# Attention into two expert layers on one core: three token blocks beside each other while the dense weights are converted, instead of two

## The chip, the core and the metric

The program runs on one core of a Trainium2 chip. The core has five engines that run their own instruction lists in order and wait for each other by semaphores: TensorE (PE, matrix products into PSUM), VectorE (DVE), ScalarE (ACT), GpSimd (POOL) and SyncE (SP), which here only issues transfers. PSUM has eight banks of 128 x 512 fp32 values. The metric is the device time of one execution in microseconds, as the median of several runs.

## The reference

What is computed, cut to its core (sizes put in):

```python
# q, k, v: (8, 8, 576, 64) fp32
k_p, v_p = mean of 8 neighbouring rows of k and v          # 72 keys per head
attn = softmax(q @ k_p.T / 8);  a = attn @ v_p             # (8, 8, 576, 64)
x = a.transpose(0, 2, 1, 3).reshape(4608, 512)
h = x @ moe_w_in                                           # 512 -> 2048
x = maximum(0.01 * h, h) @ moe_w_out                       # 2048 -> 512
logits = x @ moe2_w_gate                                   # 8 experts
e = argmax(logits);  p = softmax(logits)[e]                # one expert a token
out[token] = p * (relu(x @ moe2_w1[e]) @ moe2_w2[e])
```

The dense weights `moe_w_in` and `moe_w_out` arrive as 64-bit floating point, everything else as fp32.

## The kernel before

The 4608 tokens are 18 **blocks** of 256 (`NB`, two tiles `t` of 128 each). For a block the dense layer has 16 **steps** `f` (`NF`): `g1(b, f)` makes 128 columns of h with 12 products of 256 columns (L426) into one of the PSUM banks called h, ScalarE writes 0.01 h to an SBUF tile `g` (L123), VectorE takes the maximum (the relu, L433) and writes it back over h in PSUM; `g_hi` (ScalarE) and `g_lo` (VectorE, L126) split it into a high and a low fp32r part in `ghl`; `g2(b, f)` multiplies these by 128 rows of the second weight with six products of 512 columns (L453) into the block's two accumulator banks called y. All products are done as three of such parts, for accuracy.

One entry (b, f) of the list `seq` is a **slot**; there are 288. In every slot the order on each engine is: `g1` of this slot, `g_lo` of the slot before (in the first part of the program), the slot's hooks (`run_slot`), `g2` of the slot two back, the weight conversion (`conv`), `g_hi`. Nothing reorders this: the order is written by hand (`manual_schedule`), and hooks are put into slots by `at(slot, function, ...)` and `plan()`.

**Weight conversion.** There are 32 pieces of raw weight of 512 KB, two kinds times 16 steps. `w_load64` fetches a piece into one of seven buffers `r64` on SP's queue. `w_conv1` takes two ScalarE steps (L391, L392) and four VectorE steps (L393, L396, L399, L402) to turn 64-bit words into fp32 words; `w_conv2` splits them with a ScalarE copy (L123) and a VectorE subtraction (L126) into the resident weight tiles w. Step f of a block needs pieces 2f and 2f+1, so the first blocks can go no faster than the pieces come. For this reason `seq` runs blocks 0 and 1 beside each other, block 1 four steps behind (`LAG`): slots 0 to 31 are these two, and block 2 starts at slot 32. Two pieces are converted per step of block 0, up to slot 25.

**Attention.** The tiles t = 0 to 35 go through `att_a` (transposes), `att_b` (scores and maximum), `att_e` (exp), `att_n` (normalise), `att_c` (transpose, split), and `att_av(b)` makes a block's x from two tiles. `kv_load`, `kv_pool` and `kv_use` prepare keys and values of a batch. Before the first slot tiles 0, 1 and batch 0 are done; tiles 2 and 3 stand in slots 0 to 3, batch 1 in slots 4 to 16, tiles 4 and 5 in slots 16 to 29, and `att_av(2)` in slot 31.

**PSUM.** Banks a0, a1 serve attention, the gate and all transposes (`pt("att")`); h0, h1 serve h; y0, y1 are the accumulators of block 0 and later of every block from 2 on; y2, y3 are those of block 1 and join the h banks in slot 38, step 6 of block 2.

**After a block.** `y_evac` copies the accumulators to the one tile `y4` and stores them; gate logits of block 0 come from TensorE (`y_tr` with eight transposes, `y_logit`), those of all others from VectorE (`logit`, 16 instructions L473 a block, on a table `wg` that is loaded when the start-up pool is closed at the end of block 1). `route_a`, `route_b`, `route_c` write the token lists. From slot 34 on, 128 chunks of the expert weights are split (`ps_load`, `ps_split`, `ps_store`), one every 1.8 slots. The expert layer follows the last slot.

Of the kernel before, what the change touches and what calls it, by code (L numbers as in the profile page):

```python
# [21 lines left out]
def kernel(  # L22
# [12 lines left out]
    nc = tc.nc  # L35
# [4 lines left out]
    LAG = 4  # L40
# [309 lines left out]
    def att_av(b):  # L350
        for g in range(2):
# [64 lines left out]
    w_raw, w_mid, w_cnt = {}, {}, [0]  # L416
# [395 lines left out]
    for i in range(NF + LAG):  # L812
        if i < NF:
            seq.append((0, i))
        if i >= LAG:
            seq.append((1, i - LAG))
    seq += [(b, f) for b in range(2, NB) for f in range(NF)]
# [6 lines left out]
    def plan():  # L824
        for t in range(4, NT // P):
# [34 lines left out]
        for b in range(NB - 1):  # L860
            s = (b + 1) * NF + 1
            lg_at = []
            if b == 0:
                at(30, y_evac, 0)
                at(31, y_tr, 0, 0)
                at(32, y_tr, 0, 1)
                at(33, y_logit, 0)
                r = (34, 36)
            elif b == 1:
                ev, r = 37, (46, 48)  # L870
                lg_at = [38 + j // 2 for j in range(16)]
# [31 lines left out]
    def y_tr(b, i):  # L903
# [3 lines left out]
        tg = (("qT", 1), ("q", 1))[i] if b == NB - 1 else ("kv", 2)  # L907
        yT[i] = sb([P, KD, P], F32, *tg)
# [11 lines left out]
    with tc.manual_schedule():  # L920
        stack = ExitStack()
        start = stack.enter_context(tc.tile_pool(name="start", bufs=1))
        x1 = start.tile([P, KD * 2 * BLK], F32R, name="x1")
        ebias = sb([P, 1], F32, "ebias")
        nc.vector.memset(ebias, -114688.0 * 65536.0)
        e_t = [start.tile([P, 512], U32, name=f"e{i}") for i in range(2)]
# [7 lines left out]
        x_of = {1: x1.rearrange("p (k h n) -> p k h n", k=KD, h=2)}  # L934
        w_todo = [(j, f) for f in range(NF) for j in range(2)]

        def xs(b):
            return x_of.get(b, x_v)

        def load2():  # L940
            for _ in range(2):
                if w_todo:
                    w_load64()
# [27 lines left out]
        w_conv1(0, 0)  # L971
# [179 lines left out]
```

## Time and profile before

| | us |
|---|---|
| median of 3 runs | 1569.42 (1568.0 to 1576.46) |
| the profiled execution, its own time | 1575.01 |
| its span, first to last instruction | 1573.2 |
| busy: PE, DVE, ACT, POOL in the span | 1478.4, 929.4, 643.2, 329.6 |
| granted TensorE clock, mean | 0.977 of full speed |

The page of the profile also cuts the span into 40 slices of 39.3 us. PE's busy tenths rise from 4 in the first slice to 9 in the eighth and stay there to the last but one; DVE's are 9, 8, 9 in the second to fourth slice, fall to 7, and are 8 up to the middle of the span. A matmul's busy time includes its way through the array, so the weight loads (PEld), which have no such overlap, are the better measure of how densely PE is fed. The expert layer takes the last third of the span with PE alone near its limit.

### The profile page before, as it was taken

To read this page: it belongs to the slowest core of one execution; us is meant where nothing else is said; L and a number is where in the kernel's file an instruction comes from. 1 tells how busy PE (TensorE), PEld (TensorE's weight loads), DVE (VectorE), ACT (ScalarE), POOL (GpSimd) and SP (SyncE) were. 2 spreads that over 40 slices of the span, in tenths; PEclk is the share of its full clock that TensorE was granted. 3 is DMA by queue.
4 is the path that set the end of the run, shared out by engine and by line. 5 is a ranking of instruction groups with operands and counts; after the bars stand their busy time and mean duration, and the time that the engine had idled before them with its cause. 6 is when DMAs were issued, how large, how long until landed. Compare 5 with 4: busy or idle time off the path is not lost. (4 is left out here: it accounts for less than half of the span.)

```text
span 1573.2 us, 25017 instructions
## 1 busy us (share of the span) xinstructions
PE 1478.4 (94%) x8778; PEld 1292.1 (82%) x8778; DVE 929.4 (59%) x2393; ACT 643.2 (41%) x1444; POOL 329.6 (21%) x290
## 2 busy tenths in 40 slices
PE   4567899999999999999999999999999999999998
PEld 3456689999898888899889899987888888888886
DVE  6989748978788879877878878653111111111111
ACT  4655544445444454544445444322222222222222
POOL 3000002232332233222222333021111111121111
PEclk8787999999999999999999999999999999999999
DMA  8533035656555555545636554054721331661160
GB/s 208 159 108 102 28 127 174 183 166 196 152 178 170 180 160 184 179 157 166 198 135 198 165 162 160 28 212 160 292 111 48 147 145 41 228 278 46 61 235 22
DMA packets 113280, 238.01 MB, mean 151 GB/s; under 512 B 47589, under 2 KB 55785, under 8 KB 109440
## 3 DMA queue, kind: packets, MB, share of 16 engines
q1 hardware_dynamic: 82208, 139.81, 28.5%
q10 hardware_dynamic: 23328, 76.56, 13.1%
q0 software_dynamic: 7616, 20.01, 3.9%
q8 instruction: 71, 1.16, 0.4%
q14 instruction: 57, 0.47, 0.2%
HBM read 418.44 MB, written 87.38 MB: 322 GB/s over the span
## 5 line engine op out<-in xcount | busy, mean ns | idle before, releaser
L453 PE MATMUL y<-w,ghl 128*128 128x512 f32 x1728 | 464.3, 406 | 0.4 <-DVE ghl L126 0.2
L453 PEld LDWEIGHTS y<-w,ghl 128*128 128x128 f32 x1728 | 311.0, 192 | 56.5 <-DVE ghl L126 1.7
L426 PEld LDWEIGHTS h<-x_t,w 128*128 128x128 f32 x1776 | 237.5, 196 | 58.9 <-issue 21.7
L426 PE MATMUL h<-x_t,w 128*128 128x256 f32 x1776 | 245.6, 289 | 40.8 <-ACT ghl L123 21.4
L126 POOL TENSOR_TENSOR ps<-ps 128x512 f32<-128x512 f32 x128 | 182.7, 1427 | 479.8 <-ACT ps L123 356.5
L473 DVE CUSTOM_DVE_ANT_0 junk<-y,wg 128x512 bf16<-128x512 f32 x256 | 197.9, 773 | 1.9
L426 PEld LDWEIGHTS y<-x_t,w 128*128 128x128 f32 x1488 | 189.6, 188 | 9.4
L426 PE MATMUL y<-x_t,w 128*128 128x256 f32 x1488 | 192.1, 280 | 0.0
L126 DVE TENSOR_TENSOR at_t<-a,at_t 128x512 fp32r<-128x512 f32 x76 | 52.4, 689 | 203.8 <-ACT at_t L123 203.6
L126 DVE TENSOR_TENSOR vm<-a,vm 128x512 fp32r<-128x512 f32 x40 | 27.7, 692 | 199.7 <-ACT vm L123 199.7
L123 ACT ACTIVATE g<-h 128x256 f32<-128x256 f32 x164 | 62.9, 383 | 173.0 <-PE h L426 162.4
L433 DVE TENSOR_TENSOR h<-g,h 128x256 f32<-128x256 f32 x164 | 69.5, 424 | 91.6 <-ACT g L123 91.0
L797 PE MATMUL y<-w,at_t 128*128 128x512 f32 x480 | 120.8, 400 | 1.4 <-ACT at_t L123 0.9
L805 POOL DMA_INDIRECT out_dram<-kv,sidx x40 | 40.3, 1008 | 382.7 <-ACT vm L123 192.3
L797 PE MATMUL y<-w,vm 128*128 128x512 f32 x480 | 120.3, 400 | 0.0
L771 PE MATMUL h<-w,x_t 128*128 128x512 f32 x480 | 118.5, 396 | 0.0
L771 PE MATMUL y<-w,x_t 128*128 128x512 f32 x480 | 118.4, 395 | 0.0
L123 ACT ACTIVATE ghl<-h 128x256 fp32r<-128x256 f32 x164 | 62.7, 382 | 111.3 <-PE y L453 46.7
L797 PEld LDWEIGHTS y<-w,at_t 128*128 128x128 f32 x480 | 88.6, 188 | 22.0 <-ACT at_t L123 1.2
L797 PEld LDWEIGHTS y<-w,vm 128*128 128x128 f32 x480 | 88.7, 188 | 20.1
L771 PEld LDWEIGHTS h<-w,x_t 128*128 128x128 f32 x480 | 88.7, 188 | 18.8 <-DVE x_t L126 0.4
L771 PEld LDWEIGHTS y<-w,x_t 128*128 128x128 f32 x480 | 88.6, 188 | 18.4
(238 smaller groups left out, 1906.4 us busy)
## 6 DMA issues: line engine op xcount, KB each, us to landing
w<-wsp SPq DMA_DIRECT2D x156, 2048.0 KB
wsp<-ps ACTq DMA_DIRECT2D x128, 512.0 KB
ps<-in_moe_w_dram SPq DMA_DIRECT2D x128, 256.0 KB
y_d<-y ACTq DMA_DIRECT2D x18, 512.0 KB
q<-in_q_dram SPq DMA_DIRECT2D x28, 256.0 KB
kv<-in_k_dram SPq DMA_DIRECT2D x24, 288.0 KB
kv<-in_v_dram SPq DMA_DIRECT2D x24, 256.0 KB
ps<-in_moe_w_in_dram SPq DMA_DIRECT2D x8, 512.0 KB
```

What stands on the lines that cost most here:

```text
L123: nc.scalar.activation(o, i, AF.Copy, scale=scale)
L126: eng.tensor_tensor(out=o, in0=a, in1=b, op=ALU.subtract)
L426: nc.tensor.matmul(p[:, 0:BLK], win(f)[:, kk, l], xv[:, kk, r], start=(n == 0), stop=(n == 3 * KD - 1))
L433: nc.vector.tensor_tensor(out=g, in0=t, in1=g, op=ALU.max)
L453: nc.tensor.matmul(y_ps[b, i], hl[:, l, i * P:i * P + P], wout(f)[:, r], start=(f == 0 and l + r == 0), stop=(last and l == 1),)
L473: nc.vector.tensor_tensor_reduce(out=jk, in0=y_sb[b][:, i], in1=wg_t[0][:, e], scale=1.0, scalar=0.0, op0=ALU.mult, op1=ALU.add, accum_out ...
L771: nc.tensor.matmul(p, xT2[:, t % 2, kk, l], wlane(lane(t), fh * KD + kk)[:, r], start=(n == 0), stop=(n == 3 * KD - 1))
L797: nc.tensor.matmul(p, d[:, kk, l], wlane(lane(t), 2 * KD + 4 * j + kk)[:, r], start=(j == 0 and n == 0), stop=(j == 1 and n == 11),)
L805: nc.gpsimd.indirect_dma_start(out=out, out_offset=bass.IndirectOffsetOnAxis(ap=sidx[:, t:t + 1], axis=0), in_=o, in_offset=None, bounds_c ...
```

## The change

- `seq` holds three blocks beside each other (`NQ = 3`), each three steps behind the other (`LAG = 3`): slot 9 + 3(i - 6) begins step i from 6 to 15, with (0, i), (1, i - 3), (2, i - 6). The 48 slots of three blocks are slots 0 to 47. Pieces are converted two per step of block 0, now up to slot 34, and the second of a pair goes one slot later than the first.
- Block 2 has its own x tile (`x2`), and its accumulators are a0, a1. So from slot 11 to 39 there is no bank for attention: tiles 4 and 5, all of batch 1 and `att_av(2)` are moved up to slots 1 to 10. After block 0 is evacuated (slot 39) `pt("att")` uses y0, y1. Blocks from 3 on accumulate in y2, y3, and a0, a1 join the h banks at slot 50.
- In blocks 0 to 2 the relu is written to the SBUF tile `g` instead of back to PSUM, and `g_hi`, `g_lo` read it there.
- The raw weights have five buffers instead of seven. The conversion's `e` tiles move into `y4`.
- Blocks 0, 1 and 2 are evacuated in slots 39, 46 and 48, and all three get their logits from TensorE (tile `yT` in `x1`'s place). The start-up pool is closed at slot 54, the table `wg` loaded then. Expert chunks start at slot 38 instead of 34.

```diff
-    LAG = 4
+    LAG = 3
+    NQ = 3
...
         t = sb([P, BLK], F32, "g", 2)
-        g = p[:, 0:BLK]
-        act_copy(t, g, 0.01)
-        nc.vector.tensor_tensor(out=g, in0=t, in1=g, op=ALU.max)
+        h = p[:, 0:BLK]
+        g = t if b < NQ else h
+        act_copy(t, h, 0.01)
+        nc.vector.tensor_tensor(out=g, in0=t, in1=h, op=ALU.max)
...
-                y_ps[b, i] = bank(f"y{2 * (b == 1) + i}")
+                y_ps[b, i] = bank(("y0", "y1", "y2", "y3", "a0", "a1")[2 * min(b, 2) + i] if b < NQ else f"y{2 + i}")
...
+    for i in range(NF + (NQ - 1) * LAG):
+        seq += [(b, i - b * LAG) for b in range(NQ) if 0 <= i - b * LAG < NF]
+    seq += [(b, f) for b in range(NQ, NB) for f in range(NF)]
...
+        for t, ss in ((4, (5, 6, 6, 7, 8)), (5, (7, 8, 8, 9, 10)), (6, (40, 41, 42, 42, 44)), (7, (42, 43, 44, 45, 46))):
+            for fn, c in zip((att_a, att_b, att_e, att_n, att_c), ss):
+                at(c, fn, t)
+            at(ss[0], q_load, t + 1)
+        at(10, att_av, 2)
+        at(47, att_av, 3)
...
+            if b < NQ:
+                e = (44, 47, 50)[b]
+                if b < NQ - 1:
+                    at((39, 46)[b], y_evac, b)
+                at(e, y_tr, b, 0)
+                at(e + 1, y_tr, b, 1)
+                at(e + 2, y_logit, b)
+                r = (e + 3, e + 5)
...
-        r64.append(sb([P, 1024], I32, "y4"))
-        r64.append(start.tile([P, 1024], I32, name="r64"))
         r64 += [sb([P, 1024], I32, "kv", 2) for i in range(2)]
...
+        def conv2(n):
+            w_conv2(n % 2, n // 2)
+            if n + 5 < 2 * NF:
+                w_load64(n + 5)
...
-        for i, c in enumerate((6, 8, 10, 12, 14, 15, 16)):
-            at(c - 2, kv_pool, 1, i)
+        for i, c in enumerate((2, 3, 4, 5, 6, 7, 8)):
+            at(c - 1, kv_pool, 1, i)
             at(c, kv_use, 1, i)
...
+        for n in range(2, 2 * NF):
+            c = slot[0, n // 2 - 1] + (n % 2 if n >= 2 * LAG + 2 else 0)
+            cv_at.setdefault(c, []).append(n)
...
-            if (b, f) == (2, 6):
-                banks["h"] += ["y2", "y3"]
+            if (b, f) == (NQ, 2):
+                banks["h"] += ["a0", "a1"]
...
+            if s == slot[0, NF - 1] + 3:
+                banks["att"] = ["y0", "y1"]
+            if (b, f) == (NQ, 6):
                 stack.close()
```

TensorE in the middle of the conversion. Before, slots of block 0 (x_t, accumulators y0 and y1) and block 1 (x1, y2 and y3) take turns:

```order
L426 MATMUL h1_997<-x_t_67,w02_872 128x256 x12
L453 MATMUL y0_508<-w12_907,ghl_958 128x512 x2
L453 MATMUL y1_509<-w12_907,ghl_958 128x512 x2
L453 MATMUL y0_508<-w12_907,ghl_958 128x512
L453 MATMUL y1_509<-w12_907,ghl_958 128x512
L426 MATMUL h0_1039<-x1_102,w01_572 128x256 x12
L453 MATMUL y2_748<-w11_576,ghl_995 128x512 x2
L453 MATMUL y3_749<-w11_576,ghl_995 128x512 x2
L453 MATMUL y2_748<-w11_576,ghl_995 128x512
L453 MATMUL y3_749<-w11_576,ghl_995 128x512
```

After, at the same place (the six products have the line number 454 there):

```order
L426 MATMUL h1_1048<-x_t_67,w01_611 128x256 x12
L454 MATMUL y2_756<-w10_324,ghl_1021 128x512 x2
L454 MATMUL y3_757<-w10_324,ghl_1021 128x512 x2
L454 MATMUL y2_756<-w10_324,ghl_1021 128x512
L454 MATMUL y3_757<-w10_324,ghl_1021 128x512
L426 MATMUL h0_1083<-x1_102,w01_611 128x256 x12
L454 MATMUL a0_1100<-w10_324,ghl_1046 128x512 x2
L454 MATMUL a1_1101<-w10_324,ghl_1046 128x512 x2
L454 MATMUL a0_1100<-w10_324,ghl_1046 128x512
L454 MATMUL a1_1101<-w10_324,ghl_1046 128x512
L426 MATMUL h1_1120<-x2_103,w00_292 128x256 x12
```

A third block (x2, accumulators a0 and a1) has come between the two, with 18 more products per step.

VectorE at the same places. Before, every slot of this part holds a relu, a lo subtraction and one conversion (and pooling of batch 1 in some):

```order
L433 TENSOR_TENSOR h_884<-g,h_884 128x256
L126 TENSOR_TENSOR ghl<-h_842,ghl 128x256
L126 TENSOR_TENSOR w_907<-y_111,w_907 128x512
L393 SCALAR_TENSOR_TENSOR e_106<-kv,e_106 128x512
L396 TENSOR_SCALAR kv<-kv 128x512
L399 SCALAR_TENSOR_TENSOR kv<-kv 128x512
L402 TENSOR_TENSOR kv<-kv,e_106 128x512
L433 TENSOR_TENSOR h_919<-g,h_919 128x256
L126 TENSOR_TENSOR ghl<-h_884,ghl 128x256
```

After (relu L434, subtractions L127):

```order
L434 TENSOR_TENSOR g<-g,h_1083 128x256
L127 TENSOR_TENSOR ghl<-g,ghl 128x256
L127 TENSOR_TENSOR w_1108<-ps,w_1108 128x512
L393 SCALAR_TENSOR_TENSOR y_106<-kv,y_106 128x512
L396 TENSOR_SCALAR kv<-kv 128x512
L399 SCALAR_TENSOR_TENSOR kv<-kv 128x512
L402 TENSOR_TENSOR kv<-kv,y_106 128x512
L434 TENSOR_TENSOR g<-g,h_1120 128x256
L127 TENSOR_TENSOR ghl<-g,ghl 128x256
L434 TENSOR_TENSOR g<-g,h_1145 128x256
L127 TENSOR_TENSOR ghl<-g,ghl 128x256
```

Two slots of three hold a conversion, the third holds a relu and a lo subtraction only; the relu writes g, and the pooling has gone from here.

SP's queue at the start, raw weight pieces (L379, L381) among the loads of batch 1. Before:

```order
L379 DMA r_112<-in_moe_w_in_dram 128x4x256
L198 DMA w_328<-in_k_dram 72x4x512 x2
L381 DMA kv<-in_moe_w_out_dram 128x1024
L205 DMA w_332<-in_v_dram 64x4x512 x2
L210 DMA w_332<-in_v_dram 8x512 x8
L379 DMA kv<-in_moe_w_in_dram 128x4x256
```

After:

```order
L379 DMA kv<-in_moe_w_in_dram 128x4x256
L381 DMA ps<-in_moe_w_out_dram 128x1024
L379 DMA ps<-in_moe_w_in_dram 128x4x256
L199 DMA w_328<-in_k_dram 72x4x512 x2
L206 DMA w_331<-in_v_dram 64x4x512 x2
L211 DMA w_331<-in_v_dram 8x512 x8
```

Two pieces that reuse a buffer (ps) now stand ahead of the keys and values of batch 1; each of the two waits for the conversion that empties its buffer.

## Rows read from the trace of the kernel before

**Rows 1.** Four stretches: each engine's busy time (instructions), granted clock, DMA share, GB/s.

```profile
43.13:102.81 59.68, 35.87 (x174) 30.77 (x175) 54.33 (x106) 34.18 (x66) 0.00 (x0) 0.79 0.43 134
102.81:181.60 78.79, 59.60 (x326) 49.99 (x324) 73.14 (x146) 48.87 (x100) 2.56 (x4) 0.88 0.27 84
181.60:269.10 87.50, 84.06 (x569) 75.58 (x569) 56.41 (x168) 35.50 (x85) 12.41 (x9) 1.00 0.38 123
269.10:323.01 53.91, 53.10 (x362) 48.70 (x362) 44.78 (x115) 27.72 (x70) 15.56 (x12) 1.00 0.58 170
```

**Rows 2.** Timeline of DVE (start, duration, instruction, idle before): relus of slots 0, 48.

```profile
43.13 0.42 DVE L433 TENSOR_TENSOR h<-g,h 128x256 f32<-128x256 f32 x1
...
269.10 0.43 DVE L433 TENSOR_TENSOR h<-g,h 128x256 f32<-128x256 f32 x1 [1.27 <-ACT g L123]
```

**Rows 3.** Waits of DVE, 43 to 182 us: total, times, longest.

```profile
DVE h L433 <- ACT g L123: 4.3, 3, 3.5
```

**Rows 4.** Waits of PE, 43 to 182 us.

```profile
PE h L426 <- ACT ghl L123: 21.4, 9, 3.3
```

**Rows 5.** Waits of PE's weight loads, 182 to 270 us.

```profile
PEld h L426 <- DVE ghl L126: 5.4, 6, 2.0
```

**Rows 6.** Timeline of DVE, slot 7 before: relu, lo, conversion, next relu.

```profile
99.03 0.42 DVE L433 TENSOR_TENSOR h<-g,h 128x256 f32<-128x256 f32 x1
...
99.69 0.68 DVE L126 TENSOR_TENSOR w<-kv,w 128x512 fp32r<-128x512 f32 x1
100.30 0.68 DVE L393 SCALAR_TENSOR_TENSOR e<-ps,e 128x512 uint32<-128x512 uint32 x1
...
102.81 0.42 DVE L433 TENSOR_TENSOR h<-g,h 128x256 f32<-128x256 f32 x1
```

**Rows 7.** Timeline of DVE: attention's steps n and b, then c, of two tiles.

```profile
52.09 0.74 DVE L322 TENSOR_REDUCE st<-pr 128x8 f32<-128x576 f32 x1
...
54.06 0.45 DVE L312 TENSOR_REDUCE w<-a 128x4 f32<-128x288 f32 x1
...
55.77 0.68 DVE L126 TENSOR_TENSOR w<-r,w 128x512 fp32r<-128x512 f32 x1
...
62.67 0.68 DVE L126 TENSOR_TENSOR at_t<-a,at_t 128x512 fp32r<-128x512 f32 x1
...
63.83 0.75 DVE L322 TENSOR_REDUCE w<-w 128x8 f32<-128x576 f32 x1
```

**Rows 8.** All pooling (L225) in the conversion stretch: busy time of DVE, POOL, clock, DMA.

```profile
43.13:181.60 138.47, 9.26 (x21) 0.00 (x0) 0.84 0.34 105
```

**Rows 9.** Groups of DVE instructions, 40 to 185 us: values' low parts.

```profile
L253 DVE SCALAR_TENSOR_TENSOR vm<-w,vm 64x128 fp32r<-64x128 f32 x4 | 1.1, 282 | 0.0
```

**Rows 10.** Timeline of DVE: first subtraction of att_av(2) in slot 31.

```profile
206.23 0.69 DVE L126 TENSOR_TENSOR x_t<-a,x_t 128x512 fp32r<-128x512 f32 x1 [1.22 <-ACT x_t L123]
```

**Rows 11.** Timeline of PE's weight loads: one slot with nothing else, 186.08 to 189.21.

```profile
186.08 1.59 PEld L426 LDWEIGHTS h<-x_t,w 128*128 128x128 f32 x12
187.61 1.23 PEld L453 LDWEIGHTS y<-w,ghl 128*128 128x128 f32 x6
189.21 0.89 PEld L426 LDWEIGHTS h<-x,w 128*128 128x128 f32 x7 [0.37 <-DVE ghl L126]
```

**Rows 12.** Timeline of PE's weight loads: transposes, logits of block 0, scores of a tile.

```profile
212.18 0.47 PEld L906 LDWEIGHTS a<-ident,y 128*128 128x128 f32 x4
...
215.40 1.87 PEld L915 LDWEIGHTS a<-wgk,kv 128*128 128x128 f32 x16
...
218.56 1.04 PEld L306 LDWEIGHTS a<-kT,qT 128*128 128x128 f32 x8
```

**Rows 13.** Timeline of ACT and DVE: a conversion's ScalarE steps, then DVE's first step.

```profile
36.08 0.66 ACT L123 ACTIVATE w<-ps 128x512 fp32r<-128x512 f32 x1
...
37.33 0.72 ACT L392 ACTIVATE e<-junk,ebias 128x512 uint32<-128x512 uint16 x1
...
38.09 0.69 DVE L393 SCALAR_TENSOR_TENSOR e<-ps,e 128x512 uint32<-128x512 uint32 x1 [0.31 <-ACT e L392]
```

**Rows 14.** DMA in 105.56 to 109.0 us: one raw piece, issued at 105.56.

```profile
DMA packets 144, 0.52 MB, mean 152 GB/s; under 512 B 16, under 2 KB 16, under 8 KB 144
```

More of the change, by code (lines that the diff above doesn't have):

```diff
@@ L453, in g2 @@
             nc.tensor.matmul(
-                y_ps[b, i], hl[:, l, i * P:i * P + P], wout(f)[:, r], start=(f == 0 and l + r == 0),
+                y_ps[b, i], hl[:, l, i * P:i * P + P], wout(f)[:, r], start=(first and l + r == 0),
                 stop=(last and l == 1),
@@ L790, in m_g2 @@
         if j == 0:
-            o_ps[t] = bank(f"y{t % 2}")
+            o_ps[t] = bank(f"y{2 + t % 2}")
         p = o_ps[t]
@@ L811 @@
     seq = []
[L812 to L817, printed above, removed]
+    for i in range(NF + (NQ - 1) * LAG):
+        seq += [(b, i - b * LAG) for b in range(NQ) if 0 <= i - b * LAG < NF]
+    seq += [(b, f) for b in range(NQ, NB) for f in range(NF)]
+    slot = {x: s for s, x in enumerate(seq)}
     NSLOT = len(seq)
@@ L824, in plan @@
     def plan():
-        for t in range(4, NT // P):
+        for t, ss in ((4, (5, 6, 6, 7, 8)), (5, (7, 8, 8, 9, 10)), (6, (40, 41, 42, 42, 44)), (7, (42, 43, 44, 45, 46))):
[4 more added lines that the diff above has]
+        at(47, att_av, 3)
+        for t in range(8, NT // P):
             b, i = divmod(t, TPB)
@@ L834, in plan @@
             at(s + 5, att_c, t)
-        for b in range(2, NB):
+        for b in range(4, NB):
             at((b - 1) * NF + NF - 1, att_av, b)
@@ L862, in plan @@
             lg_at = []
[L863 to L871, printed above, removed]
+            if b < NQ:
[6 more added lines that the diff above has]
+                r = (e + 3, e + 5)
             elif b == NB - 2:
-                ev, r = None, (s + 9, s + 11)
+                r = (s + 9, s + 11)
                 lg_at = [s + j // 2 for j in range(16)]
             else:
-                ev, r = None, (s + 15, s + 19)
+                r = (s + 15, s + 19)
                 lg_at = [s + max(j - 1, 0) for j in range(16)]
-            if b == 1:
-                at(ev, y_evac, b)
             for j, x in enumerate(lg_at):
@@ L906, in y_tr @@
             nc.tensor.transpose(p[:, kk * P:kk * P + P], y_sb[b][:, i, kk * P:kk * P + P], ident)
-        tg = (("qT", 1), ("q", 1))[i] if b == NB - 1 else ("kv", 2)
-        yT[i] = sb([P, KD, P], F32, *tg)
+        if b == NB - 1:
+            yT[i] = sb([P, KD, P], F32, ("qT", "q")[i])
+        else:
+            if i == 0:
+                yT["both"] = start.tile([P, TPB, KD, P], F32, name="yT", tag="x1")
+            yT[i] = yT["both"][:, i]
         act_copy(yT[i], p.rearrange("p (k n) -> p k n", k=KD))
@@ L933, with conv1 @@
         alt = sb([P, 4096], F32, "w02")
[L934 to L943, printed above, removed]
+        for b, x in ((1, x1), (2, x2)):
+            x_of[b] = x.rearrange("p (k h n) -> p k h n", k=KD, h=2)
+        def conv1(n):
+            w_conv1(n % 2, n // 2)
+        def conv2(n):
+            w_conv2(n % 2, n // 2)
+            if n + 5 < 2 * NF:
+                w_load64(n + 5)
         kv_load0_k(0)
@@ L948 @@
         kv_load0_v(0)
-        load2()
-        load2()
+        for n in range(4):
+            w_load64(n)
         q_load(2)
         q_load(3)
-        w_load64()
+        w_load64(4)
         consts()
```

83 lines of the change are left out of this document (38 added, 45 removed).

## The prediction

> **What bounds the kernel now.** I read the program by stretches, cut where VectorE starts a slot's relu [rows 1, 2]. In the first two (slots 0 to 7 and 8 to 23) DVE is busy 54.3 of 59.7 us and 73.1 of 78.8 us, PE's weight loads only 30.8 and 50.0. Whether DVE is the bound, the waits say: from 43 to 182 us it waits 4.3 us in all for a relu's input [rows 3], while PE waits 21.4 us for h banks that ScalarE still reads [rows 4]. So 24 slots take 138.5 us, the pace of the conversion on DVE. From 181.6 us on it is PE: weight loads 75.6 of 87.5 us, clock 1.00, and the waits left are 5.4 us, for an h bank that VectorE's lo subtraction still reads [rows 5]. The conversion stretch is where PE has room; the total of products in the program hardly changes, so what the change can win is PE's idle time there.
>
> **The change, part by part.** I add up the time at which slot 48 (step 0 of block 3) has its relu, since after it both programs do nearly the same. Before, that is 269.1 us; slot 0 has its relu at 43.1 us [rows 2], and what lies ahead of that holds the same instructions in both.
>
> *Slots 0 to 10 (DVE's pace).* Prices are from start to start. Relu and lo take 0.66 (99.03 to 99.69) and a conversion 3.12 (99.69 to 102.81) [rows 6]. The new slots 0 to 10 hold 14 conversions (43.7 us), 11 relus and lo's (7.3), four attention tiles, of which tiles 4 and 5 are moved up, at 3.68 (52.09 to 55.77) plus 1.16 (62.67 to 63.83) each (19.4) [rows 7], four subtractions of two `att_av` at the 0.61 (99.69 to 100.30) of an equal subtraction (2.4) [rows 6], and all of batch 1: pooling 9.3 [rows 8], eight low parts at 0.28 [rows 9] and under a microsecond of small ones (together 12.2). Sum 85.0. In slots 3 and 10 `att_c` and `att_av` of a block now stand in one slot with nothing between on DVE, as in slot 31 before, where the subtraction waits 1.2 us [rows 10]: four such waits, 4.9. The 3.5 us wait of before, for an h bank held by relu and split [rows 3, 4], goes: the relu now leaves the bank at once. Slot 11: 43.1 + 85.0 + 4.9 = 133.0 us. From below, the waits are hidden (128); from above, twice as long (138).
>
> *Slots 11 to 35 (eight rounds of three slots).* A round costs DVE two conversion slots of 3.78 and one of 0.66, 8.2 us. It costs PE three slots of 2.76: twelve loads 1.53 and six 1.23, with the 0.37 of waiting left out [rows 11], 8.3 us. The two are so near that each will wait for hand-overs. One: ScalarE does a conversion's copy, Abs and Relu in order, and DVE's first conversion step starts 2.01 us after that copy (36.08 to 38.09) [rows 13], while DVE's own relu, lo and subtraction take 0.66 + 0.61 = 1.27 [rows 6]. In the first conversion slot of a round, ahead of which DVE had little to do, this leaves about 0.6 of waiting. Two: the next 0.01 h needs one of two g tiles, free only after a lo subtraction of 0.42; I put 0.5 on that. An estimate of 9.3 us a round, 74.6 in all: slot 35 at 207.6. The ends are 8.3 (no hand-over shows) and 10.5 (below, the clock).
>
> *Slots 35 to 48 (PE's pace).* PE is then a slot ahead of DVE. Twelve slots at 2.76 are 33.1. Beside them: tiles 6 and 7 at about 2.1 each, half of it scores [rows 12], `att_av(3)` 1.9, logits of block 0 with 2 x 0.47 + 1.87 = 2.8 [rows 12], one set of transposes of block 1 0.5, one more `g2` 1.2 [rows 11], small ones 0.7: 11.3. I add 1.6 for waits: the 5.4 us of before came from lo subtractions that read the bank [rows 5], which no longer do. Together 46.0, so slot 48 at 253.6, **15.5 us** sooner.
>
> *After slot 48.* Blocks 1 and 2 now take their logits from PE, 2.8 each, 5.6, of which 0.5 was counted: **5.1 us** back, since PE is full there (53.1 of 53.9 us busy) [rows 1]. What DVE is spared covers nothing on the path. Blocks from 3 on accumulate and evacuate as before.
>
> *At nothing.* A raw piece has landed 3.4 us after its issue (144 packets between 105.56 and 109.0) [rows 14]; with five buffers it is issued four slots ahead of its use, some 12 us. If that cover went, each of 26 pieces would stall ScalarE and DVE. Keys and values of batch 1 now queue on SP behind two pieces that wait for conversions, but these conversions end before slot 0 and DVE wants the keys in slot 1, some 8 us later. `y_evac(2)` waits on ScalarE for the store of block 1 out of the same y4, two slots earlier, with g_hi of slot 48 and the next 0.01 h queued behind it; the store moves as much as a raw piece, so I take it as landed.
>
> Net: 15.5 - 5.1 = 10.4 us. The profiled execution took 1575.0 us, 5.6 over the median of 1569.4; the same difference off the median gives **1559 us** (1564.6 for a profiled one like it).
>
> **The rivals.**
>
> *The clock.* PE's clock was 0.79 and 0.88 of full speed in the two DVE-bound stretches and 1.00 once PE was fed densely [rows 1]. If the three-block stretch keeps 0.79, a PE slot costs 2.76 / 0.79 = 3.5 and a round 10.5, 9.6 us more in eight rounds: 1569, no change. At 0.88 a round is 9.4 and nothing changes. For it: DVE still sets half of the pace. Against: PE is then busy for about nine tenths of a round, against 0.63 (50.0 of 78.8) by its loads before. The Trainium skill, TensorE: Matmul & The Clock Gate, section Part 1: The HAM clock gate, says that the throttled state is the default and that activity releases it; by that rule the stretch runs at full clock, and these traces agree (1.00 from 181.6 us on).
>
> *Two h banks until slot 50 (the slower side).* Before, two more banks joined h at slot 38, now at slot 50, and in the whole stretch g1 turns on h0, h1 alone. If the two banks, not the bank's reader, set the pace, slots 11 to 48 go no faster than the 24 slots after the conversion did, 87.5 / 24 = 3.65 us [rows 1]: 37 x 3.65 = 135, slot 48 at 268, and the 5.1 on top make 1573.5, slower by 4. It decides from 3.54 us a slot up (mine: 3.26); slower by over 0.5% needs 3.75. For it: PE's largest wait is for h banks [rows 4]. Against: the wait named is for readers that the relu to SBUF removes, and the 3.65 carries attention that the stretch has not.
>
> *Hidden hand-overs.* DVE and ScalarE work ahead where PE lags, a round costs 8.3, eight of them 8 us less: 1551.
>
> *A starved conversion.* Pieces or keys come late after all: at 1 us for each of 26 pieces, 1585.
>
> **How the numbers follow.** Forecast 0.56 (1559, from 1549 to 1567 with the front's ends and half of the round's), hidden hand-overs 0.15, clock 0.11, two banks 0.13, starved 0.05. The range leaves out the outer part of the first and the last two: 1548 to 1570. 0.5%, about what a measurement of this kernel can tell from no change, is 7.8 us, so faster means under 1561.6. Of the forecast about 0.4 lies there, all of the hidden hand-overs and 0.04 of the rest: faster 0.59. Slower (over 1577.3): the starved case and the upper part of two banks, 0.10. The same: 0.31.
>
> **What would show it.** Right: slot 48's relu near 254 us; rounds of 9 to 9.6 us from about 133 us on; clock near 1.00 in them; no wait of PE for a bank that g_hi or g_lo reads; slots 48 to 63 some 5 us longer. Wrong: slot 11 later than 138 us (front), rounds over 10 us with clock under 0.9 (clock), PE waiting for relus at full clock (banks), ScalarE waiting for raw pieces (starved), or a stretch after slot 64 that is not as long as before.

## The result, and the profile after

The changed kernel takes 1590.74 us (median of 6, 1588.36 to 1592.47) against 1577.06 us (6 runs, 1568.0 to 1579.99) for the kernel before on the same chip: ratio 1.010, 95% interval 1.0069 to 1.0131. It is 1% slower. The forecast was 1559 us, faster; the time lies outside the range and on the other side. The forecast started from the first three runs of the kernel before, 1569.42 us; its gain of 10.4 us off the median of all six would be 1566.7, which changes nothing in this.

| | before | after |
|---|---|---|
| profiled execution, own time | 1575.01 | 1589.99 |
| its span | 1573.2 | 1588.3 |
| granted TensorE clock, mean | 0.977 | 0.967 |
| relu of slot 0 / 48 / 64 | 43.1 / 269.1 / 323.0 | 43.1 / 276.9 / 347.5 |
| last relu | 1057.9 | 1072.9 |

Set against the forecast stretch by stretch, cut at the relus it named, the loss is in three places, and the middle of the change is not one of them (the sum of the last column is the 25.4 us between 1564.6, the forecast for a profiled execution, and 1590.0):

| stretch | forecast | after | difference |
|---|---|---|---|
| to slot 11 | 133.0 | 146.9 | +13.9 |
| slots 11 to 35 | 74.6 | 74.1 | -0.5 |
| slots 35 to 48 | 46.0 | 55.9 | +9.9 |
| slots 48 to 64 | 59.0 | 70.6 | +11.6 |
| slot 64 to the last relu | 734.9 | 725.4 | -9.5 |

Four stretches of the changed kernel, as [rows 1]: window, its length, then busy time (instructions) of PE, PEld, DVE, ACT, POOL, granted clock, DMA share, GB/s.

```profile
43.05:146.92 103.87, 63.71 (x307) 55.68 (x308) 82.25 (x168) 49.20 (x102) 1.12 (x2) 0.69 0.35 97
146.92:221.00 74.08, 69.49 (x434) 59.88 (x433) 60.99 (x121) 43.77 (x92) 0.60 (x2) 1.00 0.29 90
221.00:276.89 55.89, 52.14 (x332) 46.97 (x331) 28.28 (x81) 23.82 (x55) 7.04 (x5) 0.94 0.32 102
276.89:347.53 70.64, 65.15 (x409) 59.26 (x408) 41.28 (x122) 28.79 (x75) 18.97 (x16) 0.90 0.53 167
```

In the first, VectorE should set the pace and is busy only 82 of 104 us; in the last two TensorE should, and its clock is no longer 1.00.

**The front (slots 0 to 10).** Waits of DVE from 43 to 147 us (total, times, longest), beside the 4.3 us of [rows 3] and 2.5 us in smaller rows of that view, from 43 to 182 us:

```profile
DVE x L127 <- ACT x L124: 10.1, 4, 4.0
DVE y L393 <- ACT y L392: 4.5, 5, 2.1
DVE w L127 <- ACT w L124: 2.6, 2, 1.3
DVE st L313 <- PE a L307: 1.0, 1, 1.0
DVE g L434 <- ACT g L124: 0.4, 1, 0.4
```

18.6 us. The four waits for x are the two `att_av` of slots 3 and 10, the kind of [rows 10]; there one cost 1.2 us. Timeline of DVE in slot 10 (start, duration, instruction, idle before and its releaser), then the clock of that stretch:

```profile
138.56 0.69 DVE L127 TENSOR_TENSOR x<-a,x 128x512 fp32r<-128x512 f32 x1 [4.01 <-ACT x L124]
141.98 0.69 DVE L127 TENSOR_TENSOR x<-a,x 128x512 fp32r<-128x512 f32 x1 [2.72 <-ACT x L124]
```

```profile
129.20:146.30 17.10, 13.65 (x57) 12.55 (x58) 9.53 (x18) 4.70 (x9) 0.00 (x0) 0.50 0.19 62
```

Half of `att_av(2)` takes 3.4 us at the lower of TensorE's two clock levels, and VectorE has nothing between the two halves. One wait for `y` is a late raw piece. SP's queue, then ACT:

```profile
40.48 15.16 SPq L211 DMA_DIRECT2D w<-in_v_dram  x8
```

```profile
61.48 0.66 ACT L391 ACTIVATE junk<-ps 128x512 bf16<-128x512 bf16 x1 [8.02 <-DMA ps<-in_moe_w_out_dram]
```

Eight small loads of batch 1's values took 15 us to issue, and the next raw pieces stood behind them.

**The rounds (slots 11 to 35)** are as forecast. DVE in one round:

```profile
187.60 0.42 DVE L434 TENSOR_TENSOR g<-g,h 128x256 f32<-128x256 f32 x1 [0.53 <-ACT g L124]
...
189.47 0.69 DVE L393 SCALAR_TENSOR_TENSOR y<-ps,y 128x512 uint32<-128x512 uint32 x1 [0.51 <-ACT y L392]
...
192.00 0.41 DVE L434 TENSOR_TENSOR g<-g,h 128x256 f32<-128x256 f32 x1
...
195.79 0.41 DVE L434 TENSOR_TENSOR g<-g,h 128x256 f32<-128x256 f32 x1
...
197.07 0.42 DVE L434 TENSOR_TENSOR g<-g,h 128x256 f32<-128x256 f32 x1 [0.54 <-ACT g L124]
```

9.47 us, with the two hand-overs that the prediction named, at 0.5 us each. PE's 21 us of waiting for a bank that ScalarE reads [rows 4] have no row in this stretch any more; PEld waits from 147 to 221 us for the lo part alone:

```profile
PEld y L454 <- DVE ghl L127: 9.1, 13, 1.2
```

**Slots 35 to 48.** Weight loads, as [rows 12]:

```profile
251.04 0.42 PEld L910 LDWEIGHTS y<-ident,y 128*128 128x128 f32 x4 [1.54 <-DVE at_t L127]
...
260.48 0.14 PEld L242 LDWEIGHTS y<-ident,kv 72*128 72x128 f32 x1 [1.48 <-DVE at_t L127]
260.93 2.20 PEld L923 LDWEIGHTS y<-wgk,yT 128*128 128x128 f32 x16 [0.31 <-DVE rm_t L127]
263.01 2.25 PEld L454 LDWEIGHTS a<-w,ghl 128*128 128x128 f32 x6
265.36 2.89 PEld L426 LDWEIGHTS h<-x,w 128*128 128x128 f32 x12
```

PE returns to the attention banks y0, y1 before VectorE has emptied them. From 262.4 us on six loads take 2.25 and twelve 2.89 us instead of 1.23 and about 1.6: the clock has halved. In the whole stretch the weight loads wait 4.9 us.

**Slots 48 to 64.** The chain that added most, in slot 57 (8.3 us from relu to relu; 4.4 before), across engines:

```profile
315.33 0.15 DVE L541 CAST six<-rmx 128x1 int32<-128x1 f32 x1
...
316.69 0.97 POOL L542 DMA_INDIRECT lst<-ent,six  x1 [8.96 <-DMA kv<-in_v_dram]
317.68 1.29 POOL L127 TENSOR_TENSOR ps<-ps 128x512 f32<-128x512 f32 x1
319.00 0.34 ACTq L703 DMA_DIRECT2D wsp<-ps  x1
319.44 0.38 ACT L124 ACTIVATE ghl<-a 128x256 fp32r<-128x256 f32 x1 [7.58 <-POOL ps L127]
...
319.87 1.35 PEld L454 LDWEIGHTS y<-w,ghl 128*128 128x128 f32 x5 [2.13 <-ACT ghl L124]
```

The routing of block 2, now this early, puts its indirect transfer ahead of an expert chunk on GpSimd; the chunk's store holds ScalarE's queue, and `g_hi` behind it holds PE. The row of the indirect transfer names a transfer of batch 2's values as what ended its 8.96 us of waiting, so the loads crowded into these slots have a part in the chain too. The four stretches of slots 35 to 64 in which the clock was at its lower level:

```profile
262.40:269.20 6.80, 6.80 (x28) 6.22 (x28) 0.38 (x2) 0.80 (x2) 0.00 (x0) 0.50 0.63 224
282.80:286.20 3.40, 3.40 (x17) 3.40 (x17) 0.92 (x3) 0.77 (x2) 1.19 (x2) 0.51 0.41 122
320.40:323.80 3.40, 3.40 (x13) 2.96 (x12) 2.38 (x7) 1.94 (x6) 0.31 (x1) 0.50 0.39 99
337.50:344.30 6.80, 6.80 (x26) 6.13 (x26) 2.06 (x4) 2.13 (x5) 1.28 (x1) 0.50 0.12 49
```

20.4 us at half speed, so some 10 us lost by an estimate from these rows (half of the time, where PE was never idle). Before, these slots ran at 1.00 [rows 1].

### The profile page after: what moved, and what is told of

Read it like the earlier page. It is cut to its first block, busy times and chain, and to the rows that moved or that the text cites. A ratio compares the mean times of both kernels' runs of the same rounds, so it can differ in the third digit from the quotient of the medians.

```text
span 1588.3 us, 25075 instructions
## 1 busy us (share of the span) xinstructions
PE 1489.4 (94%) x8826; PEld 1303.9 (82%) x8826; DVE 913.6 (58%) x2331; ACT 644.2 (41%) x1448; POOL 325.8 (21%) x290
## 5 line engine op out<-in xcount | busy, mean ns | idle before, releaser
L454 PE MATMUL y<-w,ghl 128*128 128x512 f32 x1632 | 440.8, 407 | 7.0 <-DVE ghl L127 5.0
L454 PEld LDWEIGHTS y<-w,ghl 128*128 128x128 f32 x1632 | 292.4, 192 | 62.6 <-DVE ghl L127 10.0
L127 POOL TENSOR_TENSOR ps<-ps 128x512 f32<-128x512 f32 x128 | 181.2, 1416 | 472.6 <-ACT ps L124 415.1
L426 PEld LDWEIGHTS h<-x_t,w 128*128 128x128 f32 x1656 | 219.5, 194 | 26.8 <-DVE w L127 13.7
L426 PE MATMUL h<-x_t,w 128*128 128x256 f32 x1656 | 224.7, 286 | 13.8 <-DVE w L127 12.9
L426 PEld LDWEIGHTS a<-x_t,w 128*128 128x128 f32 x1416 | 180.4, 188 | 9.0
L426 PE MATMUL a<-x_t,w 128*128 128x256 f32 x1416 | 182.7, 280 | 0.0
L127 DVE TENSOR_TENSOR at_t<-y,at_t 128x512 fp32r<-128x512 f32 x70 | 48.2, 688 | 204.3 <-ACT at_t L124 204.1
L127 DVE TENSOR_TENSOR vm<-y,vm 128x512 fp32r<-128x512 f32 x40 | 27.7, 692 | 199.7 <-ACT vm L124 199.7
L773 PE MATMUL a<-w,x_t 128*128 128x512 f32 x480 | 118.4, 395 | 0.0
L773 PEld LDWEIGHTS a<-w,x_t 128*128 128x128 f32 x480 | 88.6, 188 | 18.4
L434 DVE TENSOR_TENSOR h<-g,h 128x256 f32<-128x256 f32 x122 | 51.7, 424 | 63.2 <-ACT g L124 62.8
L124 ACT ACTIVATE ps<-ps 128x512 fp32r<-128x512 f32 x128 | 80.4, 628 | 18.6 <-DMA ps<-in_moe_w_dram 8.4
```

Of the source, the lines that this page charges most:

```text
L124: nc.scalar.activation(o, i, AF.Copy, scale=scale)
L127: eng.tensor_tensor(out=o, in0=a, in1=b, op=ALU.subtract)
L426: nc.tensor.matmul(p[:, 0:BLK], win(f)[:, kk, l], x[:, r], start=(n == 0), stop=(n == 3 * KD - 1))
L434: nc.vector.tensor_tensor(out=g, in0=t, in1=h, op=ALU.max)
L454: nc.tensor.matmul(y_ps[b, i], hl[:, l, i * P:i * P + P], wout(f)[:, r], start=(first and l + r == 0), stop=(last and l == 1),)
L773: nc.tensor.matmul(p, xT2[:, t % 2, kk, l], wlane(lane(t), fh * KD + kk)[:, r], start=(n == 0), stop=(n == 3 * KD - 1))
```

## The experiments

Times are medians; each ratio is to the kernel before, run on the same chip. The median of the kernel before was 1575.2 to 1580.2 us on these chips, so a few us between two medians can be the chip; the ratios are free of that. Positions are relus in the profiled execution, one for each program: e3, e8 and e11, alike up to slot 50, reach slot 11 at 138.8 to 140.1 and slot 48 at 267.3 to 270.0 us.

| | us | ratio (95%) | slot 11 | 35 | 48 | 64 | 64 to last relu |
|---|---|---|---|---|---|---|---|
| before | 1577.06 | 1 | 116.9 | 223.9 | 269.1 | 323.0 | 734.9 |
| the change | 1590.74 | 1.0069-1.0131 | 146.9 | 221.0 | 276.9 | 347.5 | 725.4 |
| e1_relu_psum | 1605.53 | 1.0175-1.0225 | 146.4 | 233.0 | 288.3 | 359.9 | 728.6 |
| e2_before_sbuf | 1570.55 | 0.9956-0.9994 | 114.2 | 213.1 | 258.8 | 314.3 | 739.0 |
| e3_front_spread | 1582.37 | 1.0031-1.0086 | 138.8 | 212.9 | 267.3 | 338.9 | 726.4 |
| e4_logits2_dve | 1589.64 | 1.0064-1.0118 | 147.3 | 221.5 | 277.4 | 346.6 | 728.3 |
| e5_tail_spread | 1587.21 | 1.0045-1.0097 | 139.3 | 215.0 | 264.9 | 339.2 | 732.0 |
| e6_values_later | 1582.72 | 1.0024-1.0067 | 136.9 | 211.1 | 265.4 | 337.4 | 728.3 |
| e7_all | 1573.10 | 0.9954-0.9999 | 138.6 | 214.4 | 264.3 | 325.1 | 729.4 |
| e8_route2_later | 1579.79 | 0.9991-1.0042 | 139.4 | 213.5 | 267.8 | 335.3 | 729.5 |
| e9_sbuf_chunks38 | 1565.74 | 0.9894-0.9944 | 114.1 | 214.3 | 259.8 | 315.6 | 730.8 |
| e10_after_chunks43 | 1605.76 | 1.0144-1.0194 | 147.4 | 221.2 | 276.6 | 345.0 | 735.7 |
| e11_chunk_gap | 1579.45 | 0.9990-1.0024 | 140.1 | 214.3 | 270.0 | 329.8 | 734.1 |

**The relu, undone and alone.** e1_relu_psum, from the changed kernel:

```diff
-        g = t if b < NQ else h
+        g = h
```

> The changed kernel with one part undone: the relu goes back over h in PSUM in all blocks. Theory one (the relu in SBUF frees the h banks early and is a part that works): with h0 and h1 alone until slot 50 the lo subtraction, one slot later, holds the bank again; the three-slot rounds between the relus of slots 11 and 35 grow from 9.47 us to 9.9 or more, slots 35 to 48 from 55.9 to 58 or more, the program is 5 to 15 us slower than the changed kernel (1595 to 1605). Rival (two h banks set the pace whoever reads them): rounds within 0.2 us of 9.47 and the program within 3 us of 1590.7.

Slots 11 to 35 took 86.65 us instead of 74.08, a steady round 11.1 instead of 9.47; the program is 15 us slower than the change. Theory one. The row that had gone is back (PEld, 147 to 233 us):

```profile
PEld h L426 <- DVE ghl L127: 23.5, 24, 1.8
```

e2_before_sbuf, from the kernel before:

```diff
-        g = p[:, 0:BLK]
+        h = p[:, 0:BLK]
+        g = t if b < 2 else h
...
```

> The kernel before with one part of the change alone: the relu of blocks 0 and 1 goes to the SBUF tile g. Theory one: PE's waits for h banks (21.4 us in the conversion stretch before) lie beside work of VectorE but for the one of 3.5 us, so the program gains 2 to 6 us (1571 to 1575 beside 1577). Rival one: the waits were on the path after all and 10 us or more go. Rival two: the two g tiles, now held until the lo subtraction, become the wait instead, and nothing changes or it is slower by 2 us or more.

1570.55 against 1575.23 us, 0.25% faster, as theory one had it for the program. But at slot 48 it is 10.3 us ahead, as rival one said, and 5.6 us of that goes again, most of it after slot 64. DVE now hardly waits from 43 to 182 us; its one row:

```profile
DVE g L434 <- ACT g L123: 1.8, 2, 1.3
```

So two blocks beside each other with this relu reach slot 35 at 213.1 us; the versions with three and the same relu reach it between 211.1 (e6) and 221.5 us (e4).

**The front.** e3_front_spread, from the changed kernel (the list of a slot's pieces is taken out when run, so that nothing is converted twice):

```diff
-        for t, ss in ((4, (5, 6, 6, 7, 8)), (5, (7, 8, 8, 9, 10)), ...
+        for t, ss in ((4, (4, 5, 5, 6, 7)), (5, (6, 7, 7, 8, 9)), ...
...
+        at(10, lambda: conv(10))
         at(10, att_av, 2)
...
+        at(LAG, lambda: conv(LAG))
         at(LAG, att_av, 1)
```

> The changed kernel with the front laid out otherwise: tile 4 and 5 one slot earlier, and in slots 3 and 10 the slot's weight conversion is put ahead of att_av, so that VectorE has work while TensorE makes x. Theory one (the front lost its time in VectorE's hand-over waits, 18.7 us in slots 0 to 10): slot 11's relu comes at 136 to 141 us instead of 146.9, and the program is 5 to 10 us faster than the changed kernel (1581 to 1586). Rival (TensorE at half clock, or the late raw piece, sets the front whatever the order): slot 11 within 2 us of 146.9.

Slot 11 at 138.8, the program 8.4 us faster than the change (some 6.6 by the ratios). Theory one. DVE's waits from 43 to 139 us fall to 10.5 us, and of the 10.1 us for x this is left:

```profile
DVE x L127 <- ACT x L124: 0.2, 1, 0.2
```

e6_values_later, from e3_front_spread:

```diff
-        kv_load0_v(1)
+        at(2, kv_load0_v, 1)
```

> e3_front_spread with the load of batch 1's values (1.2 MB) issued in slot 2 instead of ahead of slot 0, so that the next raw pieces and tile 4's q pass it on SP's queue. Theory one (the raw piece that slot 1 waits for, 8.0 us on ScalarE and 2.0 on VectorE, is late because SP spent 15 us on issuing those values): the two waits go, slot 11's relu comes 1.5 to 3 us sooner than 138.8, the program gains as much. Rival (the engines of the DMA are the limit, and the later load delays later pieces as much): slot 11 within 1 us of 138.8 or later.

Slot 11 at 136.9, 1.9 us sooner, and the waits for `y` fall from 3.2 to 1.3 us. But e7, which holds this edit too, has slot 11 at 138.6, and e3, e5, e8 and e11, which do not, at 138.8 to 140.1, so the 1.9 us is hardly clear of what executions differ by. The program's time did not move beyond its interval: the place of the wait is shown (in e7 too `y` waits 1.2 us only), its worth is not.

**Slots 35 to 48.** e5_tail_spread, from e3_front_spread:

```diff
-                e = (44, 47, 50)[b]
+                e = ((40, 42, 45), (47, 48, 49), (50, 51, 52))[b]
...
-        at(40, gate_rows)
+        at(45, gate_rows)
...
-            s = 38 + i * 9 // 5
+            s = 47 + i * 9 // 5
...
-                yT["both"] = start.tile([P, TPB, KD, P], F32, name="yT", tag="x1")
+                yT["both"] = (
+                    sb([P, TPB, KD, P], F32, "ps", 3) if b == 0
+                    else start.tile([P, TPB, KD, P], F32, name="yT", tag="x1")
+                )
```

> The kernel with the front laid out otherwise (e3_front_spread), and beside it: the transposes and logits of block 0 in slots 40, 42 and 45 instead of 44 to 46 (their SBUF tile takes one of the buffers of the expert chunks, which start at slot 47), the gate's rows in slot 45. No slot from 40 to 47 then asks for more than two attention banks, but slot 47 for three. Theory one (slots 44 to 47 are slow since PE comes back to y0, y1 before ScalarE and VectorE have emptied them, and its clock falls in such gaps): the stretch from slot 35 to slot 48 falls from 54.4 us to 46 to 49, the clock stays at 1.00 up to slot 48, the program is 5 to 8 us faster than e3_front_spread (1574 to 1577). Rival (the attention and the narrow products themselves are the price, wherever they stand): 53 us or more and the clock falls again behind the logits.

The stretch and the one behind it:

```profile
215.01:264.91 49.90, 48.18 (x330) 43.91 (x329) 26.34 (x81) 21.02 (x50) 0.00 (x0) 1.00 0.19 56
264.91:339.18 74.27, 67.00 (x411) 60.74 (x410) 41.39 (x122) 29.11 (x75) 19.35 (x16) 0.89 0.55 152
```

49.9 instead of 54.4 us, at full clock: 0.9 us short of theory one, far from the rival. PE's weight loads wait 2.2 us in it instead of 4.9, and the 3.5 us at half clock (254.5 to 258.0 in e3) are gone, worth half of that: together 4.4 of the 4.5 us, by an estimate from these rows. It also had no expert chunk before slot 47, so that the banks alone did it is not shown; but e10 below, which loads none before slot 43, still has both waits of 1.5 us for a bank and takes 55.3 us. The program did not gain: the next stretch gave back 2.7 us and the time after slot 64 some 5.6.

**Slots 48 to 64.** e4_logits2_dve, from the changed kernel:

```diff
-            if b < NQ:
-                e = (44, 47, 50)[b]
+            if b < NQ - 1:
+                e = (44, 47)[b]
...
+            elif b == NQ - 1:
+                r = (s + 15, s + 19)
+                lg_at = [56 + j // 2 for j in range(16)]
...
-            if (b, f) == (NQ, 6):
+            if (b, f) == (NQ, 2):
```

> The changed kernel with block 2's gate logits made on VectorE in slots 56 to 63 and its routing in slots 64 to 70, as the kernel before did; the table wg is loaded at slot 50 for it. Theory one (the loss after slot 48 is the early routing, whose indirect transfer held GpSimd, ScalarE's queue and then TensorE in slot 57, and TensorE's logits with the clock falling behind them): the stretch from the relu of slot 48 to that of slot 64 falls from 70.6 us to between 60 and 63, the program is 7 to 11 us faster than the changed kernel (1580 to 1584). Rival (VectorE's 16 logits take the path instead, or the stretch is long for the chunks of the expert weights): 66 us or more, and the program within 4 us of 1590.7.

69.2 us: the rival. Slot 57 took 5.1 instead of 8.3 us, but VectorE now ran behind PE, and the values of batch 2, for which `att_av(4)` waits, came 4.0 us late in slot 63, with the clock at half behind it. DVE, then POOL, in slot 61:

```profile
329.57 0.68 DVE L475 CUSTOM_DVE_ANT_0 junk<-y,wg 128x512 bf16<-128x512 f32 x1
...
330.29 2.63 DVE L475 CUSTOM_DVE_ANT_0 junk<-y,wg 128x512 bf16<-128x512 f32 x1
```

```profile
329.86 1.28 POOL L229 TENSOR_TENSOR kv<-kv,mask 64x512 f32<-64x512 f32 x1 [9.80 <-DVE kv L226]
331.11 1.26 POOL L127 TENSOR_TENSOR ps<-ps 128x512 f32<-128x512 f32 x1
```

e8_route2_later, from e3_front_spread:

```diff
-                r = (e + 3, e + 5)
+                r = (e + 3, e + 5) if b < NQ - 1 else (64, 68)
```

> e3_front_spread with the routing of block 2 alone moved from slots 53 to 57 to slots 64 to 70; its logits stay on TensorE. Theory one (the routing's indirect transfer in slot 57 delays GpSimd's chunk, ScalarE's store and then TensorE): slot 57 takes 4 to 5.5 us instead of 8.2 and the stretch from slot 48 to 64 falls from 71.5 us by 4 to 6. Rival (the delay only moves to the next hand-over): slot 57 is short but the stretch stays within 2 us of 71.5.

Both in part. Slot 57 fell to 3.8 us and the stretch by 4.0, to 67.5, but slot 58 now took 8.1, since the chunk itself is late. ACT:

```profile
314.31 0.63 ACT L124 ACTIVATE ps<-ps 128x512 fp32r<-128x512 f32 x1 [5.78 <-DMA ps<-in_moe_w_dram]
```

On SP's queue the chunk stands behind the table `wg` (2 MB, which the change loads in slot 54) and the values of batch 2. e11_chunk_gap, from e8_route2_later, keeps the chunks out of there:

```diff
-            s = 38 + i * 9 // 5
+            s = 38 + (i if i < 8 else i + 5) * 9 // 5
```

> e8_route2_later with no expert chunk loaded from slot 51 to 60: the first eight chunks as before, the rest nine slots later (still all of them, to slot 278). Theory one (with the routing moved, slot 58 waits 5.8 us on ScalarE for a chunk whose transfer stands on SP's queue behind the table wg, 2 MB, and the values of batch 2; the transfers crowd these slots): slots 57 and 58 take 7 to 8 us together instead of 11.8, the stretch from slot 48 to 64 falls from 67.5 to 60 to 64 us, the program is 2 to 6 us faster than e8_route2_later. Rival (the wait moves on to the next hand-over once more, as the values for att_av(4)): 65.5 us or more.

```profile
270.00:329.82 59.82, 58.04 (x406) 53.39 (x405) 35.30 (x104) 26.69 (x69) 10.27 (x9) 1.00 0.44 131
```

59.8 us at full clock, slots 57 and 58 together 6.6: theory one for the stretch. The program stayed at 1579 us: of the 7.7 us that the stretch saved beside e8, slots 0 to 48 took 2.2 more in this execution and the time after slot 64 4.6.

e7_all is e5 and e6 together, with block 2's logits on VectorE in slots 53 to 63, its routing in slots 64 to 70, `wg` loaded in slot 50 as in e4, and the values of batch 2 prepared a slot sooner:

```diff
+            if nb == 2:
+                use[4:] = [use[3] + 1, use[3] + 3, use[3] + 5]
```

> e5_tail_spread and e6_values_later together, with block 2's logits on VectorE spread over slots 53 to 63, its routing in slots 64 to 70 and the values of batch 2 prepared one slot sooner (slots 57, 59, 61). Theory one (the waits of PE from slot 48 to 64, and the halved clock behind each, came from the early routing, the logits and the values that att_av(4) waits for): slot 48 to 64 falls from 71.5 us to 57 to 61, clock 1.00 but behind block 1's logits; the program is 18 to 24 us faster than e3_front_spread (1558 to 1564), 0.7 to 1% faster than the kernel before. Rival (that stretch is bound by something these edits leave alone, as block 2's logits moved alone showed): 67 us or more, the program at 1568 or above.

The stretch took 60.8 us, as theory one said, but the program 1573.1, slower than its 1558 to 1564 and where the rival had it (1568 or above): its first stretches stayed where e5 had them, and slot 64 comes at 325.1, still behind the 323.0 of before.

**After slot 64.** e9_sbuf_chunks38 is e2_before_sbuf with

```diff
-            s = 34 + i * 9 // 5
+            s = 38 + i * 9 // 5
```

> The kernel before (two blocks beside each other) with two parts of the change alone: the relu of blocks 0 and 1 in SBUF, and the expert chunks from slot 38 instead of 34. Theory one (what the changed kernel gained after slot 64, 725.4 us against 734.9 from there to the last relu, comes from where the chunks fall against the attention: before, att_av waits 1.3 to 1.9 us for the values at 791.8 and 900.5 us and the clock halves behind it): slot 64 at 314 as in e2_before_sbuf, the rest 739 less 6 to 11, the program 4 to 9 us faster than e2_before_sbuf (1562 to 1567), 0.6% to 0.9% faster than the kernel before. Rival (the gain came from the banks, or varies from one execution to the next): the rest as in e2_before_sbuf within 3 us, the program at 1569 to 1572.

and e10_after_chunks43 the changed kernel with the same line at 43:

> The changed kernel with the expert chunks from slot 43 instead of 38: from there on they fall in the same slots as those of the kernel before, five chunks behind. Theory one (where the chunks fall decides): the time from slot 64 to the last relu is 733 to 737 us instead of 725.4, with the clock halved again near 790 to 920 us; before it slots 38 to 42 have a little less to do (0 to 2 us). The program is 5 to 10 us slower than the changed kernel (1596 to 1600). Rival (banks, or chance): that time stays within 3 us of 725.4, and the program at 1587 to 1592.

From slot 64 to the last relu, in before, the change, e9 and e10:

```profile
323.01:1057.89 734.88, 721.55 (x4824) 657.28 (x4823) 583.54 (x1628) 339.57 (x837) 202.10 (x151) 0.99 0.52 166
```

```profile
347.53:1072.92 725.39, 714.48 (x4822) 652.17 (x4821) 583.36 (x1611) 341.14 (x838) 200.50 (x150) 1.00 0.52 170
```

```profile
315.56:1046.38 730.82, 719.08 (x4824) 655.63 (x4823) 586.20 (x1629) 341.05 (x839) 204.76 (x153) 0.99 0.53 169
```

```profile
345.04:1080.78 735.74, 720.93 (x4822) 657.22 (x4821) 581.96 (x1610) 342.08 (x841) 208.17 (x154) 0.99 0.54 171
```

Moving the chunks takes 8.2 us off e2 (739.0) and puts 10.3 on the change, with all banks left alone: the times of theory one in both, and in both the interval of the program's ratio lies apart from that of the kernel it was made from. How the place of the chunks does it is not shown. Theory one named this wait of before; the 6.8 us behind it ran at clock 0.50:

```profile
791.78 0.19 PEld L365 LDWEIGHTS a<-rm_t,vr 128*128 128x128 f32 x1 [1.85 <-ACT vr L123]
```

But e8 and e11, whose chunks lie in the change's slots (from slot 60 on, e11's are five chunks behind), had the same fall at 802 and 796 us. In e11, the wait and the clock behind it:

```profile
795.35 0.19 PEld L366 LDWEIGHTS y<-rm_t,vr 128*128 128x128 f32 x1 [1.80 <-ACT vr L124]
```

```profile
796.50:803.20 6.70, 6.70 (x25) 6.02 (x25) 2.81 (x9) 2.21 (x4) 1.67 (x1) 0.50 0.09 37
```

And in e10 the clock fell elsewhere than I expected, at 446 us behind the same kind of wait. The nine versions with three blocks whose chunks lie in the change's slots, some five chunks behind, took 725.4 (the change) to 734.1 us (e11) after slot 64, nearly up to the 734.9 of before. The program e10 was 15 us slower than the change, not 5 to 10 (some 11 by the ratios; the chip of e9 and e10 gave the kernel before 1580.2 us); its profiled execution, 1599.57, is the fastest of its six, 6 us under the median, and of those no row tells. e9 is the fastest of all: ratio 0.992, interval 0.9894 to 0.9944, with two blocks beside each other.

## Why the prediction was wrong, step by step

- **Slots 0 to 10, "four such waits, 4.9".** The step that failed first. DVE's own work was right (103.9 us less 18.6 of waits is 85.3; forecast 85.0). The waits were priced from one wait at full clock, and I looked only at `att_c` beside `att_av`. Moved into the front, the attention meets TensorE at clock 0.50 (four waits 10.1 us), weight copies that stand on ScalarE behind an exp of a tile (2.6 us), and a late raw piece (2.1 us): 18.6 us of waits in place of 4.9. e3 takes 8.1 us away by putting conversions between and the two tiles one slot earlier.
- **"At nothing: a raw piece has landed 3.4 us after its issue".** The time from issue was not the cover; the issue itself was late by 15 us on SP. I had asked whether the keys were late behind the pieces, not whether the pieces were late behind the values. One piece, 2 us on DVE: small; the starved conversion of the rivals came once, not 26 times.
- **Slots 11 to 35.** Right: 9.47 us a round against 9.3, clock 1.00, no bank held by `g_hi` or `g_lo`. The rival of the clock and that of the two banks are both refuted here. (Of the two hand-overs, 2.01 less 1.27 is 0.74, where the prediction has 0.6; it measured 0.51.) e1 shows what it rests on: without the relu in SBUF the eight rounds cost 12.6 us more.
- **Slots 35 to 48, 46.0.** Mis-sized by 9.9. I added PE's instructions and 1.6 us for waits; two attention banks for up to three users a slot gave PE waits of 1.5 us, 4.9 in all, and the halved clock cost some 3.4 (half of the 6.8 us at 0.50). That is 6.7 of the 9.9. Most of the rest is in the sum of instructions: PE was not a slot ahead. The stretch holds 156 weight loads of L426, twelve for each of thirteen slots, where I counted twelve slots, and four sets of transposes where I counted three. Laid out otherwise (and without chunks), e5 takes 49.9, of which 47.7 are not waits; I had put 44.4 there.
- **After slot 48, "5.1 us back".** The term itself fits: 53.9 + 5.1 = 59.0, and e11, with block 2's routing and the chunks out of the way, takes 59.8. What I left out is what else the change puts there: block 2's routing and the table `wg`, among expert chunks and the values of batch 2. That cost 11.6 us, some 6.8 of it as half of the 13.6 us at half clock after 276.9, most of the rest in waits of the weight loads (6.5 us, 0.9 before). The routing moved alone gave 4.0 (e8), the chunks after it 7.7 (e11); `wg` was not tried by itself.
- **After slot 64, "as before".** Wrong in the other direction, by 9.5 us. e9 and e10 put the direction down to the chunks' new places; the way is open, and since 725.4 is the least of nine such layouts, part of the 9.5 may be this execution's own.
- **What the third block is worth.** The 16.3 us that I gave slot 35 (223.9 to 207.6) I put down to PE's idle time. e2 gets 10.7 of it with two blocks, and three with the front spread (e3) come no earlier, 212.9 against 213.1; with the values later (e6) they come 2.0 us earlier. In e2, DVE works from 43 to 182 us with 1.8 us of waits, since the attention stands between the conversions; three blocks take it from there, and DVE waits 10.5 us in the front and 13.1 in the rounds (e3). That is why I take it that PE's room was not to be had: DVE has much the same work to do from slot 0 to slot 35 (busy 142.8 us in e3, 145.6 in e2), and lost its filler. In all versions that I ran, three blocks stay behind two: 325.1 (e7) against 314.3 (e2) at slot 64. That no layout of three could do better is not shown.

The clock was my rival at the wrong place. The Trainium skill, TensorE: Matmul & The Clock Gate, section HAM oscillation — how this bites in real kernels, says that a wait for data lets the throttle return, so that the work behind it starts at the lower clock. The trace agrees, 0.50 in the four stretches above, though its waits, 1.0 to 2.1 us, are shorter than those of the page's example. I had applied the release of the throttle to the rounds alone, not its return to the crowded slots around them.

## What to carry to other kernels

When work is moved to free one stretch, sum the place it is moved to as carefully as the one it leaves, with the waits of every engine and with what else is on the queues there. Filler between dependent steps is worth its own time: take it away from the pacing engine and hand-overs appear that no row of before shows. And try the parts of a change alone: here the relu in SBUF and the place of the chunks (e9) gained 0.8%, and the third block, with all that was moved for it, lost more than both.

## What the chip showed that I had not expected

- TensorE's clock fell to half behind single waits of 1.0 to 4.0 us (1.01, 1.48, 1.73 and 2.13 in the changed kernel, 3.98 in e4), while 9.1 us of waits in the dense rounds (13, the longest 1.2) left it at 1.00, and so did the wait of 1.54 us at 251.0. Behind which waits it falls, these runs do not settle: PE waited for the values of an `att_av` 1.28 us at 900.5 us in the kernel before and 1.29 us at 782.8 us in e9, and the clock fell behind the first alone. Each with the clock behind it, the kernel before first:

```profile
900.51 0.19 PEld L365 LDWEIGHTS a<-rm_t,vr 128*128 128x128 f32 x1 [1.28 <-ACT vr L123]
```

```profile
902.70:906.10 3.40, 3.40 (x13) 2.97 (x13) 1.69 (x4) 1.23 (x2) 0.62 (x1) 0.51 0.00 0
```

```profile
782.75 0.19 PEld L365 LDWEIGHTS a<-rm_t,vr 128*128 128x128 f32 x1 [1.29 <-ACT vr L123]
```

```profile
782.80:790.00 7.20, 7.20 (x51) 6.66 (x52) 4.04 (x10) 2.96 (x7) 1.68 (x1) 1.00 0.19 75
```

- A VectorE instruction with two SBUF inputs was held while GpSimd worked: 2.63 us instead of 0.68, ending 0.55 us after GpSimd's second instruction (331.11 + 1.26). The Trainium skill, SBUF — State Buffer, section Who interferes with whom, calls this an exclusive lock on a shared port pair; the trace agrees, through two GpSimd instructions in a row.
- Eight loads of 16 KB took 15.2 us to issue behind 1.2 MB of keys and 1.0 MB of values; 10.3 us in the kernel before, and 8.25 us where two raw pieces and the values stand ahead of them (e6).
